# An attention and expert-routing kernel: the first expert's weights asked for ahead of the search's branch, and the logits' update placed behind the row numbers

## The chip, the cores and the metric

The kernel runs on one core of one Trainium2 chip. The metric is the time of one execution in microseconds (us) on the device, as the median of several runs. A profile is one execution more, recorded by the hardware profiler; its times count from the start of the span, the stretch from its first instruction to its last.

## The reference

Two stages follow each other. The first is block-causal attention over 8 batches and 8 heads with 576 positions of 64 numbers; its result is laid out as `x`, 4608 tokens of 512 numbers. The second is a mixture of 8 experts. Each pair (token, expert) has a logit, and the pairs are taken greedily by descending logit: a token goes to one expert, an expert takes at most `cap` = 576 tokens.

```python
logits = x @ w_gate                      # [4608, 8]
order = np.argsort(-logits.flatten())
for idx in order:
    tok, e = (int(idx) // E, int(idx) % E)
    if assigned[tok] >= 0 or counts[e] >= cap:
        continue
    assigned[tok] = e
    counts[e] += 1
for e in range(E):
    h = np.maximum(x[assigned == e] @ w1[e], 0.0)   # w1: 512 x 1024
    out[assigned == e] = h @ w2[e]                  # w2: 1024 x 512
```

## The kernel before

**Order of the work.** Both stages are written as Python generators, which a planner (`Sched`) interleaves when the program is built. Each `yield` names an engine (D VectorE, A ScalarE, T TensorE, G GpSimd, S SyncE's DMA queue), an estimated cost in ns and the events to wait for; the planner keeps a clock of each engine and picks the piece that can start first, by priority where pieces compete. So the costs and events only set the order in which instructions stand on each engine; on the chip each engine runs its own list in order and waits on semaphores.

**The experts one by one.** `Moe` does not sort. For k = 0 to 7 it finds the expert whose cap-th largest remaining logit is highest, hands that expert its tokens and takes them out. Expert k stands for the k-th one in that order, and its number is known only at run time. The steps for one expert:

- `route(k)` searches, for all experts at once, the threshold at which 576 tokens lie above it, in rounds t = 0, 1, 2, …: counting on VectorE (`jk`, L809/L810) and ScalarE (`ja`, L752), a TensorE product that sums over partitions (`tot`, L824), and VectorE again (`sg`, L827). For k = 0 alone, ahead of round 4, a test is put in (L776 to L796). It asks whether the expert with the highest lower bound already has exactly 576 tokens above it. If so, a branch (`tc.If(rv==0)`, closed at L845) skips rounds 4 to 13. With these inputs it is skipped. ScalarE, TensorE and VectorE take part in the branch; SyncE does not.
- Behind the branch VectorE marks the expert's tokens (`sm`, `d2`, `ds`, `MM`, `ge`, L849 to L863), and writes the expert's number to `eidx` (L860). `MM` has two halves: tokens above the threshold, and tokens equal to it, of which only the first are taken.
- Scans (L867) and TensorE products (`po`, L879 to L886) turn the marks into positions; `invert` turns positions into row numbers: `OH`, `OL`, `RH` (L920 to L926), products `pe` (L935), a copy `ixt` (L938), products `ps` (L942) and the copy `ix` (L945), 576 row numbers in five columns.
- `gather` lets GpSimd write five indirect DMAs that fetch the rows of `x` (`xg`, L1007), `flip` turns them with TensorE (`xt`, L1017) and copies them to `X` (L1021 ScalarE, L1022 VectorE), and `ffn` multiplies: `h` (L1057), `HH`/`HL` (L1043/L1045), `y` (L1082/L1086).
- `weights(k)` reads `eidx` on SyncE (`value_load`, L957) and queues eight DMAs of 512 KB there (L993): four pieces of w1, four of w2, called n = 0 to 7. Each piece is split into two 16-bit parts: the high part on ScalarE (L965, or L972 and L976), the low part as the difference of the raw piece and the high part, on VectorE for n < 4 of the first two experts (L967, two inputs in SBUF), else on GpSimd (L978). For k = 0 the fifth piece has an order of its own: GpSimd clears one column (L989) behind the last gather, and the fifth DMA waits for that; the other three queue behind it on SyncE.
- The `late` step (`out` with `full`; L869 to L871, L905 to L907) takes the chosen tokens and the chosen expert out of the logits `Lm` and starts `route(k+1)`. For k < 2 it is put on the planner's list when `RH` has been written (L928).

While the first expert is searched nothing else is left to do: attention is over, and no expert has rows yet. From the second expert on, search and gathers run beside the products of the expert before.

Of the kernel before, what the change touches and what calls it, by code (L numbers as in the profile page):

```python
# [8 lines left out]
F32 = mybir.dt.float32  # L9
# [3 lines left out]
OP = mybir.AluOpType  # L13
# [601 lines left out]
class Moe:  # L615
    def __init__(s,tc,nc,ctx,sc,L,xd,w1,w2,out):
        s.tc,s.nc,s.sc,s.L,s.xd,s.w1,s.w2,s.out=tc,nc,sc,L,xd,w1,w2,out
        s.NT=xd.shape[0]; s.D=w1.shape[1]; s.E=w1.shape[0]; s.F=w1.shape[2]; s.CAP=s.NT//s.E; s.C=s.NT//P
        s.NS=14; s.NSC=6; s.NX=4
        s.IFE=(mybir.EngineType.Activation,mybir.EngineType.PE,mybir.EngineType.DVE)  # L620
        s.cp=ctx.enter_context(tc.tile_pool(name="mcp",bufs=1))
        s.ident=s.cp.tile([P,P],F32,name="mident"); make_identity(nc,s.ident)
        s.am=s.cp.tile([P,8],F32,name="m_am"); s.nam=0; nc.gpsimd.memset(s.am,2.0**-50)
        s.ab=s.cp.tile([P,1],F32,name="m_ab")
        s.vm=s.cp.tile([P,s.C],F32,name="m_vm"); s.nP=s.cp.tile([P,s.C,s.E],F32,name="m_nP"); s.Lr=s.cp.tile([P,s.C,s.E],F32,name="m_Lr")
        s.W={}; s.X={}; s.ix={}; s.half={}; s.ny=0
    def consts(s):
        nc,cp=s.nc,s.cp
        yield G,700
# [82 lines left out]
    def route(s,k):  # L712
# [19 lines left out]
        else:  # L732
# [26 lines left out]


            lo=CB[:,0:1]; nw=s.zero; PBx=PB; more=None
            BC=s.BC[k%2]; f=rp.tile([P,2,8],F32,tag="f",name=f"f{k}"); m1=rp.tile([P,6],F32,tag="m1",name=f"m1{k}"); oh=f[:,1]
            def thresholds():
                ps=s.ps.tile([P,512],F32,tag="rt",name=f"bc{k}")
                th=s.ps.tile([P,512],F32,tag="tot",name=f"th{k}")
# [6 lines left out]
            for t in range(s.NS):  # L772
                w=4.0**-t
                cnt=rp.tile([P,3],F16,tag="cnt",name=f"cn{k}_{t}")
                cand=base
                if t==s.NX and k==0:  # L776
                    yield D,70
                    V.tensor_tensor(CB[:,2:3],lo,nw,op=OP.add)
                    yield T,60
                    th=s.ps.tile([P,512],F32,tag="tot",name=f"tx{k}")  # L780
                    nc.tensor.transpose(th[:,:32],CB[:32,2:3].to_broadcast([32,P]),s.ident[:32,:32]); th=th[:,0:8]
                    yield D,429
                    jk=rp.tile([P,N],F16,tag="jk",name=f"jx{k}")
                    V.tensor_scalar(jk,PB[:,:N],CB[:,2:3],0.0,op0=OP.is_lt,op1=OP.add,accum_out=cnt[:,0:1])
                    yield T,60
                    wn=s.ps.tile([P,512],F32,tag="g",name=f"wn{k}",bufs=4)[:,0:8]
                    nc.tensor.matmul(wn,lhsT=cnt[:,0:1].to_broadcast([P,P]),rhs=s.bo[:,0:8],start=True,stop=True)
                    yield D,600
                    V.tensor_reduce(m1[:,0:1],th,axis=AX.X,op=OP.max)
                    V.tensor_scalar(oh,th,m1[:,0:1],0.0,op0=OP.is_equal,op1=OP.add,accum_out=m1[:,1:2])  # L790
                    V.tensor_scalar(f[:,0],oh,m1[:,1:2],1.0,op0=OP.mult,op1=OP.is_equal)
                    V.scalar_tensor_tensor(f[:,0],wn,float(s.NT-s.CAP),f[:,0],op0=OP.is_equal,op1=OP.mult,accum_out=m1[:,1:2])
                    V.tensor_copy(BC[:,0],th)
                    rv=nc.values_load(m1[0:1,1:2].bitcast(I32),engines=s.IFE,skip_runtime_bounds_check_because="0 or the bits of 1.0")
                    more=s.tc.If(rv==0,preferred_fallthrough_block=False); more.__enter__()
                    sc.lag(1000)  # L796
                if t:
                    cand=rp.tile([P,3],F32,tag="cand",name=f"cd{k}_{t}")
                    yield D,70 if k==0 else 210,('P2',k) if PBx is not PB else None
                    if k==0: V.tensor_tensor(cand[:,2:3],base[:,2:3],nw,op=OP.add)  # L800
                    else:
                        for i in (2,0,1): V.tensor_scalar(cand[:,i:i+1],lo,nw,(i+1)*w,op0=OP.add,op1=OP.add)
                P2=s.P2 if t==s.NSC else None
                sc.add(signs(PBx,cand[:,2:3],cnt,t,P2),0,sc.now+200)
                sc.nolat()
                for i in range(2):
                    yield D,429
                    jk=rp.tile([P,N],F16,tag="jk",name=f"jk{k}_{t}_{i}")
                    if t and k==0: V.scalar_tensor_tensor(jk,base[:,i:i+1].to_broadcast([P,N]),nw,PBx[:,:N],op0=OP.add,op1=OP.is_gt,accum_out=cnt[:,i:i+1])  # L809
                    else: V.tensor_scalar(jk,PBx[:,:N],cand[:,i:i+1],0.0,op0=OP.is_lt,op1=OP.add,accum_out=cnt[:,i:i+1])  # L810
                    if i==0: sc.nolat()
                add=lambda o,a,b: V.tensor_tensor(o,a,b,op=OP.add) if k==0 else V.tensor_scalar(o,a,b,None,op0=OP.add)
                if t: add(lo,lo,nw)
                if P2 is not None:
                    V.tensor_scalar(CB[:,2:3],lo,-1.0,None,op0=OP.mult); sc.set(('nlo',k))
                    lo=CB[:,1:2]; PBx=P2
                if t==s.NS-1: add(CB[:,2:3],CB[:,0:1],lo)
                elif k==0:
                    base=rp.tile([P,3],F32,tag="base",name=f"bs{k}_{t}")
                    V.tensor_scalar(base,s.io3,w/4,lo,op0=OP.mult,op1=OP.add)  # L820
                sc.busy(D,330 if k==0 else 150)
                yield T,30,('sg',k,t)
                tot=s.ps.tile([P,512],F32,tag="tot",name=f"tot{k}_{t}")
                nc.tensor.matmul(tot[:,0:3],lhsT=s.bo,rhs=cnt,start=True,stop=True)  # L824
                yield D,72
                sg=rp.tile([P,4],F32,tag="sg",name=f"sg{k}_{t}")
                V.scalar_tensor_tensor(sg[:,0:3],tot[:,:3],s.NT-s.CAP+0.5,s.wk[:,t:t+1].to_broadcast([P,3]),op0=OP.is_le,op1=OP.mult,accum_out=sg[:,3:4])  # L827
                nw=sg[:,3:4]
                sc.lag(93)
# [15 lines left out]
            if more: more.__exit__(None,None,None)  # L845
# [3 lines left out]
            V.tensor_tensor(sm,BC,oh[:,None,:].to_broadcast([P,4,8]),op=OP.mult)  # L849
            V.tensor_tensor(d2,PV,be(oh),op=OP.mult)  # L850
            yield D,670
            V.tensor_reduce(m1[:,2:6],sm,axis=AX.X,op=OP.add)
            los,lo2s,hi2s,ei=[m1[:,i:i+1] for i in range(2,6)]
            V.tensor_reduce(ds_,d2,axis=AX.X,op=OP.add)
            u=rp.tile([P,8],F32,tag="u8",name=f"u8{k}")
            yield D,420
# [1 line left out]
            ge=rp.tile([P,C],F16,tag="ge",name=f"ge{k}")  # L858
            V.tensor_scalar(ge,ds_,los,lo2s,op0=OP.subtract,op1=OP.is_ge)
            V.tensor_copy(eidx,ei)  # L860
            sc.add(s.weights(k,eidx),1,sc.now)
            yield D,106
            V.tensor_tensor(MM[:,1],ge,MM[:,0],op=OP.subtract)  # L863
        nm=1 if last else 2
        yield D,106*nm
        for i in range(nm):
# [49 lines left out]
    def invert(s,k,L16,h2):  # L916
# [8 lines left out]
        yield D,440 if k<2 else 800  # L925
        V.tensor_tensor(RH[:,0],OH,s.tok,op=OP.mult)  # L926
        if k>1: V.tensor_scalar(RH[:,1],OH,s.pc,None,op0=OP.mult)
        else: sc.add(s.late(),0,sc.now)  # L928
        s.hold(k)
        yield T,350,'rt',('hold',k)  # L930
        tk=sc.take(); ps=s.ps.tile([P,512],F32,tag="rt",name=f"pe{k}")
# [13 lines left out]
        V.tensor_copy(ix,ps[:,:5])  # L945
        sc.set(tk)
        sc.add(s.gather(k,ix),1,sc.now); sc.set(('ix',k))
        if k==0:

            s.wu=s.ps.tile([P,512],F32,tag="g",name="warm",bufs=4)  # L950
            for n in range(s.NWU): nc.tensor.matmul(s.wu,lhsT=s.ones,rhs=OL.rearrange("p a b -> p (a b)")[:,:512],start=True,stop=True)
            sc.free[T]=max(sc.free[T],sc.now)+213*s.NWU+1500
        s.ix[k]=ix
    def weights(s,k,eidx):

        nc=s.nc; wp=s.wp; sc=s.sc
# [23 lines left out]
        for dst,src,nd,wd in ((W,s.w1,4,1024),(Y,s.w2,8,512)):  # L980
            g=1024//wd
            for d in range(0,nd,g):
                if n>=6: yield S,25,'hw',('wc',k,n-6)
                elif k>0: yield S,25,'hw',('wc',k-1,n+2),('fl',1) if k==1 and n>=4 else None
                elif n==4:

                    yield G,60,('gi',0)
                    raw=wp.tile([P,1024],F32,tag="raw",name=f"raw{k}_{wd}_{d}",bufs=6)
                    nc.gpsimd.memset(raw[:,0:1],0.0)  # L989
                    yield S,25,'hw'  # L990
                else: yield S,25,'hw'
                if k or n!=4: raw=wp.tile([P,1024],F32,tag="raw",name=f"raw{k}_{wd}_{d}",bufs=6)
                nc.sync.dma_start(out=raw.rearrange("p (g f) -> p g f",g=g),in_=src[bass.ds(e,1),d*P:(d+g)*P,:].rearrange("o (g p) f -> p (o g) f",p=P))  # L993
                hi=dst[:,0,d:d+g].rearrange("p g f -> p (g f)"); lw=dst[:,1,d:d+g].rearrange("p g f -> p (g f)")
                sc.dma(1456,('wl',k,n))
                sc.add(conv(n,raw,hi,lw,('wc',k,n)),2,sc.now)
                n+=1
    WS=32.0; XS=64.0; NWU=8; NWM=0; GW=1; GS=2; XC=()
# [151 lines left out]
```

## Time and profile before

| what | before |
|---|---|
| median of 3 runs | 793.67 us (792.71 to 794.05) |
| the profiled execution's own time | 791.57 us |
| its span | 789.8 us |
| mean granted TensorE clock in it | 0.975 |
| TensorE matmuls busy in the span | 715.5 us (91%) |
| VectorE, ScalarE, GpSimd busy | 570.4, 539.2, 466.5 us |

The profiled execution is 2.10 us below the median, and 1.77 us of it lie outside its span. Attention's last output DMA is issued at 344.23 us; the first expert's first product stands at 369.24 us. Between the two lies the stretch in which TensorE has almost nothing to do, and in it all of the changed code runs for k = 0.

### The profile page before, as it was taken

The page shows a single profiled execution, that of the slowest core. Times are in us where ns is not written, and L with a number is a line of the kernel's source. Part 1 is how long each engine was busy: PE and PEld are TensorE (multiplying, and loading weights), DVE is VectorE, ACT ScalarE, POOL GpSimd, SP SyncE. Part 2 cuts the span into 40 slices and gives each one's busy share as a digit, 9 for nine tenths or more (in the row PEclk, how much of TensorE's full clock was granted, in tenths as well). Part 3 has the DMA queues.
Part 4 walks back from the last instruction along what each step waited for, and adds up shares of the span by engine and source line. Part 5 has one row for each costly group of instructions (what it writes and reads, how often), then busy time and mean ns, then how long its engine had stood idle before and what let it go on. Part 6 is the DMA issues. An engine that isn't in the chain of part 4 may idle for free.

```text
span 789.8 us, 19021 instructions
## 1 busy us (share of the span) xinstructions
PE 715.5 (91%) x6528; PEld 476.6 (60%) x6528; DVE 570.4 (72%) x2310; ACT 539.2 (68%) x1455; POOL 466.5 (59%) x509
## 2 busy tenths in 40 slices
PE   5779998899989999936998999999999999999995
PEld 3556776667767777724545747647466475574752
DVE  6899798998899889577988978769686793620210
ACT  5788888888988898715836868594975848283210
POOL 5788888898889876413413447373763907764001
PEclk9899999999999999966999999999999999999998
DMA  9879999999998993347026076481926639851001
GB/s 202 160 150 174 214 189 224 172 151 229 205 192 178 216 181 77 91 106 252 23 98 230 8 245 150 176 199 67 279 71 220 145 103 259 260 136 41 21 20 40
DMA packets 244305, 121.51 MB, mean 154 GB/s; under 512 B 200816, under 2 KB 227312, under 8 KB 244208
## 3 DMA queue, kind: packets, MB, share of 16 engines
q1 hardware_dynamic: 238320, 101.42, 56.7%
q0 software_dynamic: 5888, 18.88, 7.6%
q8 instruction: 51, 0.84, 0.4%
q14 instruction: 46, 0.38, 0.2%
HBM read 71.32 MB, written 18.87 MB: 114 GB/s over the span
## 4 chain that ended last, share of the span: by engine, by line
PE 42%; ACT 3%; DMA 3%; DVE 3%; issue 3%; POOL 1%; SPq 0%; POOLq 0%; another core or an unknown queue 0%; ACTq 0%; DVEq 0%
PE h L1057 23%; PE y L1082 15%; PE y L1086 2%; DMA raw<-in_moe_w_dram 1%; DMA out_dram<-yo,ix 1%; DMA xg<-x,ix 1%; POOL xg L1007 1%; ACT W L976 1%; ACT ja L752 1%; ACT raw L972 1%; DVE OL L924 1%; DVE h L897 1%; PE pe L935 1%; PE tot L824 1%; DVE jk L810 0%
## 5 line engine op out<-in xcount | busy, mean ns | idle before, releaser
L438 POOL TENSOR_TENSOR P<-P,m 128x320 f32<-128x320 f32 (+8 forms) x285 | 209.5, 770 | 49.6 <-DVE m L430 32.5
L1057 PE MATMUL h<-X,W 128*128 128x320 f16 (+3 forms) x1536 | 195.7, 286 | 0.6 <-issue 0.4
L1057 PEld LDWEIGHTS <-W 128*128 128x128 f16 x1536 | 142.0, 98 | 44.3 <-issue 4.7
L416 ACT ACTIVATE P<-psb,m 128x576 f32<-128x576 f32 (+8 forms) x288 | 149.5, 543 | 27.5 <-DVE m L409 18.7
L1082 PE MATMUL y<-W,HH 128*128 128x512 f16 x512 | 152.7, 380 | 0.0
L978 POOL TENSOR_TENSOR W<-raw,W 128x1024 f16<-128x1024 f32 x56 | 118.4, 2135 | 41.6 <-ACT W L976 36.0
L405 DVE TENSOR_REDUCE m<-psb 128x1 f32<-128x576 f32 (+8 forms) x288 | 124.8, 480 | 12.3 <-PE psb L380 11.8
L463 PE MATMUL psb<-mident,P 128*128 128x128 f32 x800 | 106.3, 281 | 13.2 <-POOL P L438 5.9
L1073 POOL DMA_INDIRECT out_dram<-yo,ix x40 | 39.3, 982 | 113.7 <-ACT yo L1065 77.5
L380 PEld LDWEIGHTS <-qT 128*64 128x64 f16 x1408 | 76.6, 111 | 43.6 <-issue 28.9
L463 PEld LDWEIGHTS psb<-mident,P 128*128 128x128 f32 x800 | 87.7, 142 | 24.5 <-POOL P L438 8.5
L380 PE MATMUL psb<-kT,qT 128*64 128x288 f16 (+8 forms) x704 | 89.6, 281 | 11.7 <-ACT P L416 10.9
L498 PE MATMUL psb<-PT,V 128*64 128x448 f32 (+5 forms) x776 | 97.2, 388 | 2.3 <-DVE PT L446 1.8
L1043 ACT ACTIVATE HH<-h 128x320 f16<-128x320 f32 (+3 forms) x128 | 52.3, 411 | 67.7 <-PE h L1057 63.3
L1082 PE MATMUL y<-W,HL 128*128 128x512 f16 x256 | 97.2, 380 | 0.0
L1007 POOL DMA_INDIRECT xg<-x,ix x40 | 40.9, 1023 | 83.0 <-DVE ix L945 38.9
L1045 DVE SCALAR_TENSOR_TENSOR HL<-h,HH 128x320 f16<-128x320 f32 (+3 forms) x128 | 56.9, 452 | 42.5 <-ACT HH L1043 39.4
L444 ACT ACTIVATE PT<-psb 128x512 f32<-128x512 f32 (+1 forms) x165 | 82.6, 593 | 4.5 <-PE psb L463 4.4
L380 PE MATMUL psb<-kS,qT 128*64 128x288 f16 (+8 forms) x704 | 82.0, 278 | 1.6 <-DVE kS L350 1.4
L1082 PEld LDWEIGHTS <-HH 128*128 128x128 f16 x512 | 47.0, 98 | 51.9 <-issue 1.3
L972 ACT ACTIVATE raw<-raw 128x512 f32<-128x512 f32 x112 | 67.7, 627 | 4.5 <-DMA raw<-in_moe_w_dram 4.5
L498 PEld LDWEIGHTS psb<-PT,V 128*64 128x64 f32 x776 | 49.5, 137 | 33.4 <-issue 24.4
(216 smaller groups left out, 1044.1 us busy)
## 6 DMA issues: line engine op xcount, KB each, us to landing
raw<-in_moe_w_dram SPq DMA_DIRECT2D x64, 512.0 KB
x<-XR SPq DMA_DIRECT2D x8, 1152.0 KB
kn<-in_k_dram SPq DMA_DIRECT2D x15, 576.0 KB
qn<-in_q_dram SPq DMA_DIRECT2D x15, 576.0 KB
V<-in_v_dram SPq DMA_DIRECT2D x64, 128.0 KB
V<-in_v_dram SPq DMA_DIRECT2D x16, 64.0 KB
xg<-x,ix POOLq DMA_INDIRECT x40
out_dram<-yo,ix POOLq DMA_INDIRECT x40
```

The costliest lines, as they stand in the source:

```text
L380: nc.tensor.matmul(out if len(K1.shape) == 2 else out.rearrange("p (r j) -> p r j", r=2), lhsT=A[:, h, 64 * i:64 * i + 64], rhs=K1, start= ...
L405: nc.vector.tensor_reduce(m[:, 0, c:c + 1], ps[:, o:o + 64 * (i + 1)] if g else s.part(ps, g, i, o), axis=AX.X if g else AX.XY, op=OP.max)
L416: nc.scalar.activation(out, in_, AF.Exp, bias=m[:, 1, c:c + 1], scale=s.ESC, accum_out=m[:, 2, c:c + 1])
L438: nc.gpsimd.tensor_tensor(sl, sl, m[:, 3, c:c + 1].to_broadcast([P, w]), op=OP.mult)
L444: s.nc.scalar.activation(out, in_, AF.Copy)
L463: nc.tensor.transpose(ps[:, a], s.Pb[n % s.NP][:, s.OFF[i] + 128 * j:s.OFF[i] + 128 * j + P], s.ident)
L498: nc.tensor.matmul(ps[64 * h:64 * h + 64, 64 * (i0 - b0):64 * (b1 - b0)], lhsT=vn[:, j, 2 * (n % 2) + h, :], rhs=pt[:, s.PTI[(j, i0)]:s.PT ...
L972: nc.scalar.activation(raw[:,x],raw[:,x],AF.Copy,scale=s.WS)
L978: nc.gpsimd.tensor_tensor(lw,raw,hi,op=OP.subtract)
L1045: nc.vector.scalar_tensor_tensor(HL[:,f,ts],ps,0.0,HH[:,f,ts],op0=OP.max,op1=OP.subtract)
L1057: nc.tensor.matmul(ps,lhsT=W[:,a,d,f*P:f*P+P],rhs=X[:,4*(d//2)+d%2+l,ts],start=(d==0 and n==0),stop=(d==3 and n==2))
L1082: if m<4: nc.tensor.matmul(ps,lhsT=Z[:,f,m*P:m*P+P],rhs=Y[:,a,f],start=(f==n==0),stop=(f==7 and n==2))
```

## The change

It has two parts, and both act on the first expert (the second part on the second one too).

**Early request and early marks.** Ahead of the branch, VectorE now also works out `eidx` and the first half of `MM` as they are if the branch will be skipped, and clears the second half. `MM[:,0]` comes straight from a comparison of `PV` with the lower bounds, which are raised by 16 for the experts that are not the top one. SyncE reads `eidx` and queues the four DMAs of w1 ahead of the branch, in which it now takes part. All that stood between the branch's end and the scans (`sm` to `MM`) moves inside the branch, where it runs only if the test fails, and there the expert is read and the four DMAs are asked for once more, into the same four buffers. The planner's cost of the test's block goes from 600 to 1800.

**The late step.** For k < 2 it goes on the planner's list behind `ix` instead of behind `RH`.

```diff
-        s.IFE=(mybir.EngineType.Activation,mybir.EngineType.PE,mybir.EngineType.DVE)
+        s.IFE=(mybir.EngineType.Activation,mybir.EngineType.PE,mybir.EngineType.DVE,mybir.EngineType.SP)
...
-                    yield D,600
+                    yield D,1800
                     V.tensor_reduce(m1[:,0:1],th,axis=AX.X,op=OP.max)
+                    V.scalar_tensor_tensor(f[:,2],th,m1[:,0:1],s.io8,op0=OP.is_equal,op1=OP.mult)
+                    V.tensor_reduce(ei,f[:,2],axis=AX.X,op=OP.max)
+                    V.tensor_copy(eidx,ei)
                     V.tensor_scalar(oh,th,m1[:,0:1],0.0,op0=OP.is_equal,op1=OP.add,accum_out=m1[:,1:2])
-                    V.tensor_scalar(f[:,0],oh,m1[:,1:2],1.0,op0=OP.mult,op1=OP.is_equal)
-                    V.scalar_tensor_tensor(f[:,0],wn,float(s.NT-s.CAP),f[:,0],op0=OP.is_equal,op1=OP.mult,accum_out=m1[:,1:2])
-                    V.tensor_copy(BC[:,0],th)
+                    V.tensor_scalar(f[:,0],th,m1[:,0:1],16.0,op0=OP.is_lt,op1=OP.mult)
+                    V.tensor_scalar(f[:,2],oh,m1[:,1:2],1.0,op0=OP.mult,op1=OP.is_equal)
+                    V.scalar_tensor_tensor(f[:,2],wn,float(s.NT-s.CAP),f[:,2],op0=OP.is_equal,op1=OP.mult,accum_out=m1[:,1:2])
+                    V.tensor_tensor(f[:,0],f[:,0],th,op=OP.add)
+                    V.tensor_tensor(d2,PV,be(f[:,0]),op=OP.is_ge)
+                    V.tensor_reduce(MM[:,0],d2,axis=AX.X,op=OP.max)
+                    V.memset(MM[:,1],0.0)
+                    s.ask(eidx)
                     rv=nc.values_load(m1[0:1,1:2].bitcast(I32),engines=s.IFE,skip_runtime_bounds_check_because="0 or the bits of 1.0")
                     more=s.tc.If(rv==0,preferred_fallthrough_block=False); more.__enter__()
...
-            if more: more.__exit__(None,None,None)
...
-            sc.add(s.weights(k,eidx),1,sc.now)
+            if k: sc.add(s.weights(k,eidx),1,sc.now)
             yield D,106
             V.tensor_tensor(MM[:,1],ge,MM[:,0],op=OP.subtract)
+            if more:
+                s.ask(eidx); more.__exit__(None,None,None)
+                for n in range(4): sc.ev['wl',0,n]=sc.now+3500+1500*n
+                sc.add(s.weights(0,eidx),1,sc.now)
...
-        else: sc.add(s.late(),0,sc.now)
...
         sc.add(s.gather(k,ix),1,sc.now); sc.set(('ix',k))
+        if k<2: sc.add(s.late(),0,sc.now)
...
+    def piece(s,raw,src,e,d,g):
+        s.nc.sync.dma_start(out=raw.rearrange("p (g f) -> p g f",g=g),in_=src[bass.ds(e,1),d*P:(d+g)*P,:].rearrange("o (g p) f -> p (o g) f",p=P))
+    def ask(s,eidx):
+        e=s.nc.sync.value_load(eidx[0:1,0:1],min_val=0,max_val=s.E-1)
+        if not s.early: s.early=[s.wp.tile([P,1024],F32,tag="raw",name=f"raw0_{n}",bufs=6) for n in range(4)]
+        for n,t in enumerate(s.early): s.piece(t,s.w1,e,n,1)
```

**SyncE's list, from attention's last write to the first w2 piece.** Before, the expert's number is read once, and the eight pieces follow it:

```order
L540 DMA x<-XR_5097 128x9x512
L845 UNCONDITIONAL_BRANCH
L957 TENSOR_LOAD eidx_5267
L957 ISA x2
L993 ISA
L993 DMA raw_1024_0_5558<-in_moe_w_dram 128x1024
```

In the changed kernel the first four pieces stand ahead of the branch (`m_5270` holds the test's result), and the same request stands again inside the skipped block:

```order
L969 TENSOR_LOAD eidx_5267
L969 ISA x2
L966 ISA
L966 DMA raw_0_5362<-in_moe_w_dram 128x1024
L966 ISA
L966 DMA raw_1_5363<-in_moe_w_dram 128x1024
L966 ISA
L966 DMA raw_2_5364<-in_moe_w_dram 128x1024
L966 ISA
L966 DMA raw_3_5365<-in_moe_w_dram 128x1024
L803 TENSOR_LOAD m_5270
L872 COMPARE_AND_BRANCH
```

The read of `eidx` and the w1 requests moved from behind the marks to ahead of the branch; the w2 requests stay where they were, behind a second read of `eidx`.

**VectorE's list, from the copy `ixt` on.** Before, the six steps of the update (`m_es` to the second `m_Lm`) stand ahead of `ixt0`, and two of the four conversions of w1 behind `ix0`:

```order
L926 TENSOR_TENSOR RH0_5570<-OH0_5569,m_tok_590 128x720
L869 TENSOR_TENSOR m_es_645<-m_es_645,m10_5270 128x1
L870 TENSOR_SCALAR u80_5531<-f0_5269 128x8
L871 TENSOR_TENSOR m_Lm_644<-m_Lm_644,u80_5531 128x288
L905 TENSOR_TENSOR q0_5554<-q0_5554,MM0_5265 128x36
L906 TENSOR_SCALAR q0_5554<-q0_5554 128x36
L907 TENSOR_TENSOR m_Lm_644<-m_Lm_644,q0_5554 128x288
L938 CAST ixt0_5621<-pe0_5584 128x40
L945 CAST ix0_5633<-ps0_5624 128x5
L967 SCALAR_TENSOR_TENSOR W1_0_5545<-raw0_1024_0_5558,W1_0_5545 128x1024
L967 SCALAR_TENSOR_TENSOR W1_0_5545<-raw0_1024_1_5563,W1_0_5545 128x1024
L721 TENSOR_REDUCE m_vm_75<-m_Lm_644 128x36
```

In the changed kernel the same steps read so (L880 to L882 and L916 to L918 are the update):

```order
L948 CAST ixt0_5646<-pe0_5609 128x40
L955 CAST ix0_5657<-ps0_5648 128x5
L880 TENSOR_TENSOR m_es_645<-m_es_645,m10_5270 128x1
L881 TENSOR_SCALAR u80_5556<-f0_5269 128x8
L882 TENSOR_TENSOR m_Lm_644<-m_Lm_644,u80_5556 128x288
L916 TENSOR_TENSOR q0_5592<-q0_5592,MM0_5265 128x36
L917 TENSOR_SCALAR q0_5592<-q0_5592 128x36
L918 TENSOR_TENSOR m_Lm_644<-m_Lm_644,q0_5592 128x288
L985 SCALAR_TENSOR_TENSOR W1_0_5584<-raw0_0_5362,W1_0_5584 128x1024
L985 SCALAR_TENSOR_TENSOR W1_0_5584<-raw0_1_5363,W1_0_5584 128x1024
L985 SCALAR_TENSOR_TENSOR W1_0_5584<-raw0_2_5364,W1_0_5584 128x1024
L721 TENSOR_REDUCE m_vm_75<-m_Lm_644 128x36
```

The update moved behind `ix0`, and three conversions of w1 instead of two stand in one piece behind it.

More of the change, by code (lines that the diff above doesn't have):

```diff
@@ L625, in __init__ @@
         s.vm=s.cp.tile([P,s.C],F32,name="m_vm"); s.nP=s.cp.tile([P,s.C,s.E],F32,name="m_nP"); s.Lr=s.cp.tile([P,s.C,s.E],F32,name="m_Lr")
-        s.W={}; s.X={}; s.ix={}; s.half={}; s.ny=0
+        s.early=[]; s.W={}; s.X={}; s.ix={}; s.half={}; s.ny=0
     def consts(s):
@@ L761, in route @@
             lo=CB[:,0:1]; nw=s.zero; PBx=PB; more=None
-            BC=s.BC[k%2]; f=rp.tile([P,2,8],F32,tag="f",name=f"f{k}"); m1=rp.tile([P,6],F32,tag="m1",name=f"m1{k}"); oh=f[:,1]
+            BC=s.BC[k%2]; f=rp.tile([P,3,8],F32,tag="f",name=f"f{k}"); m1=rp.tile([P,6],F32,tag="m1",name=f"m1{k}"); oh=f[:,1]
+            los,lo2s,hi2s,ei=[m1[:,i:i+1] for i in range(2,6)]; d2=R("d2")
             def thresholds():
@@ L844, in route @@
             V.tensor_scalar(oh,f[:,0],m1[:,1:2],None,op0=OP.is_equal)
-            if more: more.__exit__(None,None,None)
             sm=rp.tile([P,4,8],F32,tag="sm",name=f"sm{k}")
-            d2=R("d2"); ds_=rp.tile([P,C],F32,tag="ds",name=f"ds{k}")
+            ds_=rp.tile([P,C],F32,tag="ds",name=f"ds{k}")
             yield D,463
@@ L852, in route @@
             V.tensor_reduce(m1[:,2:6],sm,axis=AX.X,op=OP.add)
-            los,lo2s,hi2s,ei=[m1[:,i:i+1] for i in range(2,6)]
             V.tensor_reduce(ds_,d2,axis=AX.X,op=OP.add)
@@ L982, in weights @@
             for d in range(0,nd,g):
-                if n>=6: yield S,25,'hw',('wc',k,n-6)
+                if k==0 and n<4: raw=s.early[n]
+                elif n>=6: yield S,25,'hw',('wc',k,n-6)
                 elif k>0: yield S,25,'hw',('wc',k-1,n+2),('fl',1) if k==1 and n>=4 else None
@@ L991, in weights @@
                 else: yield S,25,'hw'
-                if k or n!=4: raw=wp.tile([P,1024],F32,tag="raw",name=f"raw{k}_{wd}_{d}",bufs=6)
-                nc.sync.dma_start(out=raw.rearrange("p (g f) -> p g f",g=g),in_=src[bass.ds(e,1),d*P:(d+g)*P,:].rearrange("o (g p) f -> p (o g) f",p=P))
+                if k or n>4: raw=wp.tile([P,1024],F32,tag="raw",name=f"raw{k}_{wd}_{d}",bufs=6)
+                if k or n>3: s.piece(raw,src,e,d,g)
                 hi=dst[:,0,d:d+g].rearrange("p g f -> p (g f)"); lw=dst[:,1,d:d+g].rearrange("p g f -> p (g f)")
-                sc.dma(1456,('wl',k,n))
+                if k or n>3: sc.dma(1456,('wl',k,n))
                 sc.add(conv(n,raw,hi,lw,('wc',k,n)),2,sc.now)
```

## The prediction, made before the run

> **What bounds the kernel now.** The page comes first: TensorE's busy time in the span.
>
> ```profile
> PE 715.5 (91%) x6528; PEld 476.6 (60%) x6528; DVE 570.4 (72%) x2310; ACT 539.2 (68%) x1455; POOL 466.5 (59%) x509
> ```
>
> TensorE bounds the whole, so the change can only act where it has nothing to do: between attention's end and the first expert's products. There I read the chain that ended last, from 355 to 376 us, then the timelines of the engines, and then what TensorE waits for afterwards. The chain (start, duration, piece):
>
> ```profile
> 355.20 0.48 SPq L957
> ...
> 356.29 3.56 DMA raw<-in_moe_w_dram
> ...
> 360.07 1.07 ACT W L965
> ...
> 369.43 4.83 DMA raw<-in_moe_w_dram
> 374.29 0.63 ACT raw L972
> ...
> 375.08 0.55 ACT ja L752 x2
> ```
>
> It runs through two transfers of weights: the first piece of w1, asked for at 356.29, and later a piece of w2, issued at 369.43. Between them stand GpSimd's five gathers, of which this is the timeline:
>
> ```profile
> 361.20 1.18 POOL L1007 DMA_INDIRECT xg<-x,ix  x1 [15.87 <-ACT W L965]
> 362.69 1.73 POOL L1007 DMA_INDIRECT xg<-x,ix  x1 [0.30 <-issue]
> 364.72 0.95 POOL L1007 DMA_INDIRECT xg<-x,ix  x1 [0.30 <-issue]
> 365.97 1.53 POOL L1007 DMA_INDIRECT xg<-x,ix  x1 [0.30 <-issue]
> 367.81 0.91 POOL L1007 DMA_INDIRECT xg<-x,ix  x1 [0.30 <-issue]
> 368.71 0.12 POOL L989 MEMSET raw<- 128x1 f32 x1
> ```
>
> Read literally, the first gather waits for ScalarE's conversion of w1, so that an earlier w1 would start the gathers 3.7 us earlier. I don't believe that label: a gather needs only the row numbers `ix`. VectorE's timeline and the line's own waits decide:
>
> ```profile
> 350.56 0.16 DVE L789 TENSOR_REDUCE m<-tx 128x1 f32<-128x8 f32 x1
> ...
> 351.46 0.16 DVE L793 COPY m_BC<-tx 128x8 f32<-128x8 f32 x1
> 353.35 0.19 DVE L849 TENSOR_TENSOR sm<-m_BC,f 128x32 f32<-128x32 f32 x1 [1.73 <-DVEq L845]
> ...
> 354.86 0.14 DVE L860 CAST eidx<-m 128x1 int32<-128x1 f32 x1
> ...
> 355.08 0.35 DVE L867 TENSOR_TENSOR_SCAN SC<-m_ones,MM 128x36 f16<-128x36 f16 x2
> ...
> 358.15 0.15 DVE L869 TENSOR_TENSOR m_es<-m_es,m 128x1 f32<-128x1 f32 x1
> ...
> 359.24 0.46 DVE L907 TENSOR_TENSOR m_Lm<-m_Lm,q 128x288 f32<-128x288 f32 x1
> 359.62 0.19 DVE L938 CAST ixt<-pe 128x40 f16<-128x40 f32 x1
> 360.15 0.16 DVE L945 CAST ix<-ps 128x5 int32<-128x5 f32 x1 [0.35 <-PE ps L942]
> 361.16 2.42 DVE L967 SCALAR_TENSOR_TENSOR W<-raw,W 128x1024 f16<-128x1024 f32 x2 [0.84 <-ACT W L965]
> ...
> 365.45 1.23 DVE L967 SCALAR_TENSOR_TENSOR W<-raw,W 128x1024 f16<-128x1024 f32 x1 [1.01 <-ACT W L965]
> ```
>
> ```profile
> L1007 POOL DMA_INDIRECT xg<-x,ix x40: 907/963/1942, 361.2 to 690.9; - x40
> L1007 POOLq EVENT_SEMAPHORE  x31: 17/17/10703, 342.9 to 686.7; - x31
> ```
>
> GpSimd's queue held one wait of 10.70 us. GpSimd had been idle for 15.87, since 345.3, and `ix` ends at 360.31. A wait for `ix` fits, and 0.89 behind it the first gather starts. So the stretch is set by the chain VectorE to `ix`, then by five gathers one after the other (361.20 to 368.72, 7.52 us), then by w2 behind the last gather. TensorE shows what follows:
>
> ```profile
> 358.29 0.92 PE L935 MATMUL pe<-RH,OL 128*32 128x40 f16 x36 [2.56 <-DVE RH L926]
> ...
> 366.30 1.42 PE L1017 MATMUL xt<-m_idh,xg 128*128 128x128 f16 x16 [2.67 <-DMA xg<-x,ix]
> 368.41 1.03 PE L1017 MATMUL xt<-m_idh,xg 128*128 128x128 f16 x8 [0.69 <-DMA xg<-x,ix]
> ...
> 375.68 0.16 PE L824 MATMUL tot<-cn,m_bo 128*128 128x3 f16 x1 [1.42 <-DVE HL L1045]
> ```
>
> ```profile
> PE xt L1017 <- DMA xg<-x,ix: 2.0, 2, 1.8
> PE tot L824 <- DVE jk L810: 1.6, 2, 1.1
> PE pe L935 <- DVE RH L927: 1.4, 1, 1.4
> ```
>
> The second fence holds TensorE's largest waits from 376 to 790 us (total, times, longest). They are small, so behind the product `tot` at 375.68, the second round of the second expert's search, TensorE works nearly without a gap, and whatever moves that `tot` moves the end. It waits there for `ja` (375.08 + 0.55 = 375.63), which on ScalarE stands behind the conversion at 374.29, that is behind w2.
>
> **The change part by part.** The sum is made against the profiled execution, 791.57 us, and carried over to the median, 793.67.
>
> *The request.* `eidx` now needs three small steps behind the reduction at 350.56. At the pitch of such steps (353.35 to 355.08 holds eight steps, two of them on 288 columns) they take about 0.6, so it stands at about 351.4 instead of 355.00. From there to the first request went 1.29 (355.00 to 356.29); kept, this gives 352.7, 3.6 earlier, and the first piece lands near 356.2 instead of 359.85. This alone buys little: its readers are the conversions, and they are not what the gathers waited for. W1's own queue stays the same; w2 still stands behind the last gather, and the second read of `eidx` ahead of it finds SyncE idle.
>
> *The marks.* Behind the branch eight steps go: 353.35 to 355.08, 1.73. Ahead of it come two steps on 288 columns, like two of the eight, and five small ones net of the copy that goes, about 1.6. VectorE sat idle 1.73 between the copy and `sm`, waiting for the branch's value; part of the new steps stands behind the value, so up to 0.4 can lie beside that wait. Net −0.1 to −0.5; I take −0.15. SyncE's part in the branch costs nothing while it waits for no one but the same value: behind it lies only w2, 15 us later.
>
> *The late step.* `pe` ends at 359.21, but `ixt` starts at 359.62, since VectorE is in the update from 358.15 to 359.70 (the records overlap by a pipeline). With `ixt` free to go it starts near 359.25: −0.35. Together `ix` is 0.5 earlier (0.35 to 0.85), ending near 359.8, and the first gather starts near 360.7 by the same 0.89.
>
> *What the update and the conversions now collide with.* The median of the forty gathers is 0.963, but two of the first five took 1.73 and 1.53. Both started inside a conversion on VectorE: at 362.69 in the pair 361.16 to 363.58, and at 365.97 in the one 365.45 to 366.68. They ended 0.84 and 0.82 after that conversion's end. So such a gather waits until the conversion is over. The two that began with no conversion under way took 0.95 and 0.91. The first, recorded 0.04 behind a conversion's start, took 1.18: the edge isn't sharp. The Trainium skill, page "SBUF — State Buffer", section "Who interferes with whom", says that a VectorE operation with two SBUF inputs and a GpSimd operation that reads SBUF exclude each other for a whole instruction, and that issue order decides who waits; both rows agree, and the rule too gives one waiting gather per conversion that is under way when it is issued.
>
> In the changed kernel the update starts behind `ix`, 1.55 long (358.15 to 359.70 before), to about 361.35. The three conversions follow in one piece, 3 × 1.21 (half of 2.42) to 365.0, since w1 has landed and ScalarE has converted ahead. The gathers start at 360.7. The first (0.96) ends at 361.65; the second starts at 361.95 inside the first conversion, waits to 362.55 and ends 0.83 later, 363.4; three more at 0.30 + 0.963 each end at 367.2. Before it was 368.72: −1.5. The last conversion stands behind `X` and out of the gathers' way. W2 is issued 1.5 earlier, and the search's own branch (`PV`, `rt` behind the fourth `xt`) moves by the fourth gather's end, also about 1.5 earlier. So `tot` moves from 375.68 to about 374.2.
>
> Sum: −0.5 from `ix`, −1.0 from one stretched gather instead of two. The profiled execution would be 790.07, and the median 792.17. Its bounds: `ix` by −0.35 or −0.85 and the waiting gather by ±0.4 give −0.9 to −2.3.
>
> **The rivals.** About 0.2% of this kernel, 1.59 us, is what a measurement can tell from no change.
>
> *A, the conversions do not let GpSimd in (18%).* Three stand back to back. That a loser waits through several is seen with the engines exchanged:
>
> ```profile
> L897 DVE TENSOR_SCALAR h<-q x8: 174/182/5274, 356.3 to 669.2; 128x36 f16<-128x36 f32 x8
> ```
>
> ```profile
> 668.11 6.30 POOL L978 TENSOR_TENSOR W<-raw,W 128x1024 f16<-128x1024 f32 x3
> ```
>
> A step of VectorE whose median is 0.18 took 5.27 from 669.2 on, to the end of three operations of GpSimd (674.4). If so here, the second gather waits to 365.0, ends at 365.8, and three more end at 369.6: +0.9, 794.6. Against it: no row shows GpSimd locked out over a boundary between two VectorE operations.
>
> *B, the first gather is caught too (12%).* This is the other side. The last update step has two inputs in SBUF as well and starts at about 361.35 − 0.46 = 360.9. If the first gather, due at 360.7, comes 0.2 later relative to it, and boundaries are closed as in A, it waits to 365.0, ends at 365.8, and four more (4 × 1.263) end at 370.9: +2.2, 795.9. The point that decides is whether the gather reads ahead of 360.9.
>
> *F, the branch's instructions come late (8%).* Ahead of `sm` the chain has a piece in which VectorE waits for nothing that is shown:
>
> ```profile
> 352.84 0.52 issue
> ```
>
> No weight moves there now; w1 will. What a busy machine adds is seen in a gather's way to TensorE: the first took 361.20 to 366.30, 5.10, under w1; the third 364.72 to 368.41, 3.69; the second expert's first took even more:
>
> ```profile
> 414.36 1.00 POOL L1007 DMA_INDIRECT xg<-x,ix  x1 [4.42 <-DVE ix L945]
> ```
>
> ```profile
> 421.12 0.62 PE L1017 MATMUL xt<-m_idh,xg 128*128 128x128 f16 x8 [1.78 <-DMA xg<-x,ix]
> ```
>
> That is 6.76. Added to the chain, 1.4 to 3.1 would leave −0.1 to +1.6, say 794.4. Against it: w1's data starts about when the branch is taken. The Trainium skill, page "Runtime: NRT & Kernel Launch", section "Instruction fetch mechanics", says that a taken branch to a page not held must fetch it by DMA first; the 0.52 may be such a fetch, which no run here shows.
>
> *G, more than forecast (12%).* If no gather is caught (the first two get between the update and the conversions), five take 5 × 0.963 + 1.2 = 6.0, which is −2.0 with `ix`; and the second expert's wait of 1.78 at 421.12 may shrink by some 0.4 with its update moved: −2.4, 791.3.
>
> That the test fails is no case: the same inputs skip the block now, in the 1.73 ahead of `sm`.
>
> **How the numbers follow.** The forecast has 50%. Its own range, −0.9 to −2.3, straddles the limit of 1.59, so 24 of its 50 count as faster, 26 as the same. G adds 12 to faster; A gives 13 same and 5 slower; B 12 slower; F 4 and 4. That makes 0.36 faster, 0.43 same, 0.21 slower. The time is the forecast's, 792.2. The range goes down to 790.8, which holds most of G, and up to 795.3, which holds A and F and leaves out most of B.
>
> **What would show it.** Right: the first w1 request near 352.7; `ixt` straight behind `pe`; `ix` near 359.8; the gathers' end near 367.2 with only the second stretched, to about 1.45; `tot` near 374.2; and from there the same distance to the end as before. A shows as a second gather of about 3.8, B as a first one of about 5, F as a piece of "issue" behind the branch of over 1 us. It is wrong if the first gather starts 3 us earlier (then the label at 361.20 was right), or if `tot` moves and the end does not.

## The result: slower, and not where the change was made

| | before | after |
|---|---|---|
| median | 794.43 us (10 runs, 792.71 to 798.34) | 800.85 us (10 runs, 798.9 to 802.21) |
| ratio | | 1.0071, 95% interval 1.0049 to 1.0092 |
| profiled execution, span | 791.57, 789.8 us | 800.26, 798.2 us |

The change costs about 0.7%. The forecast was a small gain, and the range ended at 795.3; it was wrong. To find the place I set both traces against marks that lie in both. The first is the product `tx`, attention's work being over and the test just beginning; it stands 0.60 later in the profile after, a difference that arose in attention, which the change does not touch. The last mark is the product `tot` on which the prediction rested. Before and after:

```profile
350.06 0.31 PE L781 MATMUL tx<-mident,CB 32*128 32x32 f32 x1 [0.46 <-DVE CB L778]
```

```profile
350.66 0.31 PE L782 MATMUL tx<-mident,CB 32*128 32x32 f32 x1 [0.46 <-DVE CB L779]
...
375.93 0.16 PE L833 MATMUL tot<-cn,m_bo 128*128 128x3 f16 x1 [1.51 <-ACT ja L752]
```

From `tx` to `tot` it was 25.62 (350.06 to 375.68) and is 25.27: the stretch that the change edits became 0.35 shorter. From `tot` to the end of the span it was 414.1 and is 422.3. All the loss, some 8 us in this pair of executions (the medians are 6.4 apart), lies behind the edited code. TensorE's waits there show it. These are the groups in the profile after, from 376 us to the end (total, times, longest); the first holds the 1.51 at 375.93 too:

```profile
PE tot L833 <- ACT ja L752: 7.8, 6, 2.3
PE tot L833 <- DVE jk L819: 2.9, 2, 2.1
PE pe L945 <- DVE RH L938: 2.7, 1, 2.7
PE xt L1036 <- DMA xg<-x,ix: 2.3, 3, 1.7
PE h L1076 <- DMA X<-xg: 1.0, 1, 1.0
```

With 0.3 of small ones that is 17.0, or 15.5 without 375.93; before it was 6.9. The difference, 8.6, is about the loss of this pair. It is one execution of each kernel, and not every wait in it belongs to the order of the lists, as will be seen. The worst place is the turn from the second expert's last products `y` to the third one's first `h`. In the timeline of the profile after, TensorE stands in front of four things in a row:

```profile
475.90 0.38 PE L1101 MATMUL y<-W,HL 128*128 128x512 f16 x1
478.39 0.18 PE L833 MATMUL tot<-cn,m_bo 128*128 128x3 f16 x1 [2.11 <-DVE jk L819]
...
482.73 0.16 PE L833 MATMUL tot<-cn,m_bo 128*128 128x3 f16 x1 [1.18 <-ACT ja L752]
483.87 0.50 PE L1076 MATMUL h<-X,W 128*128 128x256 f16 x3 [0.98 <-DMA X<-xg]
484.94 0.16 PE L833 MATMUL tot<-cn,m_bo 128*128 128x3 f16 x1 [0.56 <-ACT ja L752]
```

Before, the same turn has no wait at all:

```profile
478.41 0.18 PE L824 MATMUL tot<-cn,m_bo 128*128 128x3 f16 x1
...
479.62 0.38 PE L1086 MATMUL y<-W,HL 128*64 128x512 f16 x2
479.94 0.83 PE L1057 MATMUL h<-X,W 128*128 128x256 f16 x6
480.60 0.17 PE L824 MATMUL tot<-cn,m_bo 128*128 128x3 f16 x1
```

Behind these waits the clock is halved. In the windows of the profile after, the first number is the length, then comes the busy time of TensorE; the granted clock stands ahead of the DMA share. In the same three windows of the profile before it was 1.00:

```profile
480.00:484.50 4.50, 2.21 (x17) 0.77 (x13) 3.42 (x23) 4.48 (x12) 4.50 (x3) 1.00 1.05 324
484.50:488.00 3.50, 3.06 (x16) 2.29 (x17) 2.56 (x15) 3.48 (x10) 3.30 (x3) 0.51 1.31 205
488.00:492.00 4.00, 4.00 (x40) 3.58 (x39) 2.69 (x16) 3.13 (x9) 4.00 (x3) 1.00 0.16 56
```

Twenty-four `h` took 4.25 there (484.96) instead of 2.78 (482.96 before), 1.5 more. In the balance of this pair that does not show, since the kernel before has such a stretch near 422 to 425 us (0.74 from 420 to 424, 0.84 from 424 to 428), where the changed one has 1.00.

**What stands there.** The lists of the engines show what the waits mean. Between `rt`, the start of the fourth expert's search, and the first `h` of the third expert, TensorE's list holds these pieces (`y*3` is three pieces of the second expert's products, 0.65 us each; `T` a search product `tot`):

```
before  rt  y*3 T  y*3 T  y*4 T  y*3 T  y*4 T  y*3 T  y*2 h h T  h*7 T
after   rt  y*4 T  y*3 T  y*3 T  y*4 T  y*3 T  y T  h T  h*8 T
```

Before, 22 pieces of `y` were left behind `rt`; now 18 are, since the search of the third expert and all that follows on it stands later on the list. The fifth and sixth round had 7 pieces together to hide behind and now have 4, and the seventh, which had 4 (two `y`, two `h`), has one `h`. A round needs VectorE's and ScalarE's turn of about 2 us (from the `tot` at 480.62 to the next at 482.73, 2.11). With one piece between two `T`, TensorE stands in front of the second.

The first wait of the four, 2.11 at 478.39, is another matter: four pieces stand ahead of that `tot`, enough for a round. VectorE's step `sg`, which reads the `tot` of 473.50, starts only at 476.73, while in the next three rounds it starts 0.2 behind the start of its `tot`:

```profile
476.73 0.16 DVE L836 SCALAR_TENSOR_TENSOR sg<-tot,m_wk 128x3 f32<-128x3 f32 x1 [3.22 <-PE y L1101]
```

Another such late start (524.92, for the `tot` of 522.19) stands ahead of the longest wait behind, 2.27 at 526.60. The kernel before has one too (519.87, for the `tot` of 518.26), so have e5 to e8 below, and e1 to e4 and e9 to e12 have none. What held `sg` is open.

### The profile page after: what moved, and what is told of

It is laid out like the page before. It is cut to its first block, busy times and chain, and to the rows that moved or that the text cites. A ratio compares the mean times of both kernels' runs of the same rounds, so it can differ in the third digit from the quotient of the medians.

```text
span 798.2 us, 19036 instructions
## 1 busy us (share of the span) xinstructions
PE 719.1 (90%) x6528; PEld 479.6 (60%) x6528; DVE 571.5 (72%) x2309; ACT 540.4 (68%) x1455; POOL 465.4 (58%) x509
## 4 chain that ended last, share of the span: by engine, by line
PE 59%; DVE 17%; ACT 8%; DMA 7%; POOL 4%; issue 4%; SPq 0%; POOLq 0%; DVEq 0%; ACTq 0%
PE h L1076 23%; PE y L1101 17%; PE psb L463 6%; DVE m L405 5%; PE psb L498 5%; PE psb L380 4%; ACT P L416 4%; DMA kT<-k 3%; DMA raw<-in_moe_w_dram 2%; DVE kS L350 2%; PE y L1105 2%; POOL P L438 2%; ACT PT L444 1%; DVE PT L446 1%; POOL xg L1026 1%
## 5 line engine op out<-in xcount | busy, mean ns | idle before, releaser
L438 POOL TENSOR_TENSOR P<-P,m 128x320 f32<-128x320 f32 (+8 forms) x285 | 209.5, 770 | 49.9 <-DVE m L430 32.8
L380 PE MATMUL psb<-kT,qT 128*64 128x288 f16 (+8 forms) x704 | 91.7, 286 | 10.4 <-ACT P L416 9.8
L380 PE MATMUL psb<-kS,qT 128*64 128x288 f16 (+8 forms) x704 | 83.8, 283 | 1.4 <-DVE kS L350 1.2
L498 PEld LDWEIGHTS psb<-PT,V 128*64 128x64 f32 x776 | 49.7, 138 | 33.1 <-issue 24.3
```

Of the source, the lines that this page charges most:

```text
L380: nc.tensor.matmul(out if len(K1.shape) == 2 else out.rearrange("p (r j) -> p r j", r=2), lhsT=A[:, h, 64 * i:64 * i + 64], rhs=K1, start= ...
L438: nc.gpsimd.tensor_tensor(sl, sl, m[:, 3, c:c + 1].to_broadcast([P, w]), op=OP.mult)
L498: nc.tensor.matmul(ps[64 * h:64 * h + 64, 64 * (i0 - b0):64 * (b1 - b0)], lhsT=vn[:, j, 2 * (n % 2) + h, :], rhs=pt[:, s.PTI[(j, i0)]:s.PT ...
```

## The experiments

All ratios are against the kernel before, run in the same set on the same chip; its median was 788.94, 796.49 and 789.52 us in the three sets (e1 to e4, e5 to e8, e9 to e12), so times of different sets are not compared. A profile is one execution each time, and the kernel before was not profiled again in these sets. There were two groups of theories: the loss is in the order of the lists behind the seam (O), or the seam itself leaves something slow behind (S).

### e1 and e2: the order moved from one kernel to the other

The planner was made to follow a list of pieces written down from the other kernel, from the product at 375.93 on; the second expert's late step stands where that list needs it.

```diff
+            if s.replay and not s.replay_off:
+                x = min(c, key=lambda y: s.rank.get(s.label(y[3]), -1))
             k, e, cost = x[3], x[5], x[6]
+            l = s.label(k)
...
+            if l == s.SWITCH:
+                s.replay = True
```

e1, the change with the order of before. 

> The changed kernel up to the second expert's second search product (tot of round 1), from there on the order of the kernel before on all engines; the second expert's late step is back behind RH, since that order asks for it. Theory O (the 8 us are lost to the order in which the planner places all that follows): TensorE's waits from 376 us on fall from about 15 us to the 7 of before, and the time is that of before less the 0.3 gained at the seam, ratio 0.997 to 1.002. Theory S (the seam does it: the early w1 transfers, the request or the clock leave something slow behind): the time stays at that of the changed kernel, ratio 1.007.

e2, the kernel before with the order of the change. 

> The mirror image: the kernel before, with its own request and marks, but from the second expert's second search product on in the order of the changed kernel; the second expert's late step therefore stands behind ix. Theory O: as slow as the changed kernel, ratio 1.006 to 1.011, with the same waits of TensorE near 478 to 485, 526, 620, 627 and 690 us. Theory S: ratio 1.000.

Measured: e1 1.0003 (0.9984 to 1.0022), e2 1.0088 (1.0059 to 1.0116). The loss goes with the order and not with the seam. e2 shows the same place, here with a longer wait for `X`, and again half clock behind it:

```profile
484.00 0.18 PE L848 MATMUL tot<-cn,m_bo 128*128 128x3 f16 x1 [0.93 <-DVE jk L834]
487.00 0.82 PE L1082 MATMUL h<-X,W 128*128 128x256 f16 x3 [2.83 <-DMA X<-xg]
```

```profile
480.00:486.00 6.00, 3.25 (x28) 1.38 (x26) 4.89 (x31) 5.69 (x14) 5.80 (x4) 1.00 0.84 220
486.00:493.00 7.00, 6.00 (x30) 4.26 (x31) 2.47 (x12) 4.63 (x12) 6.80 (x5) 0.51 1.01 220
```

The turn's two waits (0.93 and 2.83) and the 3.4 us that 7.00 us at 0.51 lose make 7.2, an estimate from these rows; the loss is 0.88% of 788.94, 6.9. So here the turn is about the whole loss. Of the other waits expected, one came (1.31 at 627.74); there is none at 526 or 620, and the one near 690 is 1.27, as in the kernel before (1.37). So the wait at 526 and what the one at 690 grew by in the profile after (2.27, and 2.67 instead of 1.37) do not follow from the order alone: e2 has the same lists there.

e1 has no wait between 430 and 567 us. Its waits came down to 9.8 and not to 7, as expected, because of one of 3.83 at 617.35, in a part whose lists are those of before:

```profile
617.35 0.16 PE L857 MATMUL tot<-cn,m_bo 128*128 128x3 f16 x1 [3.83 <-ACT ja L776]
```

The kernel before waited 0.77 at the like place. ScalarE's row says what this `ja` stands behind on its list, a conversion whose weights had not landed:

```profile
616.12 0.63 ACT L1015 ACTIVATE raw<-raw 128x512 f32<-128x512 f32 x1 [4.15 <-DMA raw<-in_moe_w_dram]
```

So a wait of that kind varies between executions of one order.

### e3 and e4: the two parts of the change alone

e3 is the kernel before with the late step behind `ix` for both experts:

```diff
-        else: sc.add(s.late(),0,sc.now)
...
+        if k<2: sc.add(s.late(),0,sc.now)
```

> The kernel before with the second part of the change alone: the late step behind ix for the first two experts, request and marks as before. Theory O: this is the part that upsets the order (the third expert's search is started later), so ratio 1.006 to 1.011. Theory S: ratio 0.999 to 1.001.

e4 is the changed kernel with that edit undone. 

> The changed kernel with the late step back behind RH for both experts: early request, early marks and the new cost alone. Theory O: the order of GpSimd's list is that of before, so ratio 0.998 to 1.003. Theory S: ratio 1.007.

Measured: e3 1.0083 (1.0055 to 1.0111), all of the loss. e4 1.0044 (1.0015 to 1.0073): a miss, neither the one nor the other. GpSimd's list is that of before, but TensorE's differs up to the fourth expert's tenth round. From 401 us on all four engines' lists are those of e6 and e10 below, which do not lose, so the order behind that is not what costs here. Its profile has a wait like that of e1, 2.77 at 620.76, behind weights that landed late, but e1 had it too and lost nothing. What e4's 0.4% is stays open.

### e5 and e6: which of the two late steps

e5 is the kernel before with the second expert's late step alone moved (`if k==1` behind `ix`), e6 the changed kernel with that step alone put back:

```diff
+        elif k==1: sc.add(s.late(),0,sc.now)
...
-        if k<2: sc.add(s.late(),0,sc.now)
+        if k<1: sc.add(s.late(),0,sc.now)
```

> The kernel before with one edit: the second expert's late step stands behind its row numbers instead of behind RH; the first expert's stretch is untouched. The third expert's search then starts about 3 us later, and GpSimd again has a scatter of the second expert ahead of the third one's gathers. Theory O1 (this step alone upsets the order behind it): ratio 1.005 to 1.010, with waits of TensorE between 478 and 490 us and a stretch of half clock behind them. Theory O2 (the planner's clock, set off by any edit at the seam, is what reshuffles the order): 0.999 to 1.002.

> The changed kernel with the second expert's late step back behind RH, the planner left to itself. Theory O1: the loss goes, ratio 0.997 to 1.004 (the request alone gave 1.004). Theory O2: ratio 1.006 to 1.009.

Measured: e5 1.0066 (1.0035 to 1.0097), e6 0.9980 (0.9958 to 1.0002). So the trigger is the second expert's late step, an edit that does not touch the first expert's stretch. In e5 that stretch is as before, and the waits between 478 and 490 us are there: 0.68, 0.93 and, for `X`, 0.97. The half clock that was expected behind them did not come: it was 1.00 from 480 to 492 us.

```profile
480.00:486.00 6.00, 4.10 (x36) 2.06 (x36) 4.96 (x31) 5.69 (x14) 5.98 (x4) 1.00 0.99 269
```

### e7 and e8: is it GpSimd's list?

In the profile after, GpSimd's gathers for the third expert start at 469.33, though the row numbers are there at 466.41: a scatter stands ahead of them.

```profile
468.06 0.96 POOL L1092 DMA_INDIRECT out_dram<-yo,ix  x1 [7.06 <-ACT m_PB L747]
469.33 0.98 POOL L1026 DMA_INDIRECT xg<-x,ix  x1 [0.30 <-issue]
```

This looked like the cause. e7 moves that one scatter behind the gathers in the changed kernel, e8 moves the gathers behind it in the kernel before; both by an edit of the list of pieces. For e7, of GpSimd's pieces:

```diff
-yev.1.1.128#2 gather.2#1 gather.2#2 gather.2#3 gather.2#4 gather.2#5
+gather.2#1 gather.2#2 gather.2#3 gather.2#4 gather.2#5 yev.1.1.128#2
```

> The changed kernel with one instruction moved on GpSimd's list: the scatter of the second expert's second output tile stands behind the third expert's five gathers instead of ahead of them; all other lists are the same. The gathers then start near 466.6 instead of 469.3. Theory G (this scatter is where the time goes: gathers late, X late, waits near 484): the wait for X near 484 goes and the time falls by 2 to 5 us against the changed kernel, ratio to before 1.001 to 1.005. Theory P (it is TensorE's list: search products that stand too late among the expert products): within 1 us of the changed kernel, ratio 1.006 to 1.009.

> The kernel before with the five gathers of the third expert moved on GpSimd's list behind the second expert's second scatter (and one conversion), nothing else moved: they start near 473 instead of 464.7. Theory G: X comes 8 us later than before, TensorE waits for it several us near 480 to 486 and loses half clock behind that: ratio 1.006 to 1.015. Theory P: there is slack of that size, ratio below 1.003.

Measured: e7 1.0062 (1.0039 to 1.0086), e8 1.0038 (1.0011 to 1.0065). e7 did what it was to do on GpSimd and bought nothing that can be measured; its ratio is in the range of theory P. Its gathers start early, the wait for `X` is gone, and TensorE waits in front of `tot` instead:

```profile
465.42 0.98 POOL L1050 DMA_INDIRECT xg<-x,ix  x1 [5.66 <-DVE bs L715]
```

```profile
474.32 0.18 PE L857 MATMUL tot<-cn,m_bo 128*128 128x3 f16 x1 [1.91 <-DVE jk L843]
...
480.99 0.18 PE L857 MATMUL tot<-cn,m_bo 128*128 128x3 f16 x1 [0.93 <-DVE jk L843]
...
483.17 0.16 PE L857 MATMUL tot<-cn,m_bo 128*128 128x3 f16 x1 [1.66 <-DVE CB L848]
```

So my first explanation (late gathers) fell for the changed kernel: without the late gathers the loss stays. What is left is TensorE's own list, where the rounds stand with too few products to hide them. That is argued from the waits and the count of pieces; no run moved the rounds alone, and the 1.91 follows a late start of `sg` (472.64, for the `tot` of 470.28), which the list does not explain. e8 lies between its two ranges, a miss for both: gathers that come 8 us late cost 0.4%, less than expected, but not nothing.

### e9 to e12: where in the order, and can it be better?

e9 follows the changed kernel's order up to the fourth expert's first `tot` and the order of before from there. 

> The changed kernel in its own order, the late third expert's search included, up to the first search product of the fourth expert (about 469 us); from there on the order of the kernel before. Theory P1 (the late search itself costs: row numbers, gathers and X of the third expert come too late for TensorE): the loss stays, ratio 1.005 to 1.010. Theory P2 (only the arrangement behind it is bad): ratio 0.998 to 1.002.

e10 repeats e6. 

> The kernel of the request and the first late step once more, since its gain stood at the edge of the interval. If the seam's gain carries to the end: ratio 0.996 to 0.999. If not: 0.999 to 1.002.

e11 puts the second expert's late step further ahead still:

```diff
-            if k>1: sc.add(out(),0,sc.now)
+            if k>0: sc.add(out(),0,sc.now)
...
-        if k<2: sc.add(s.late(),0,sc.now)
+        if k<1: sc.add(s.late(),0,sc.now)
```

> As the run before, but the second expert's late step goes still further ahead, to where the third and later experts have it (before OH). Theory P1 (the search is a chain to be started as early as possible): a little faster than the run before, ratio 0.995 to 0.999. If TensorE has slack for it already: the same as the run before; if VectorE's step in front delays the second expert's own row numbers by its 1.5 us: 1.000 to 1.003.

e12 moves the first expert's late step alone. 

> The kernel before with only the first expert's late step behind its row numbers. It frees ixt by 0.35 us and moves the update in front of the conversions. Expected from the seam alone: ratio 0.999 to 1.001, and no new wait of TensorE behind 430 us.

Measured: e9 1.0040 (1.0011 to 1.0069), e10 1.0008 (0.9982 to 1.0034), e11 1.0184 (1.0146 to 1.0221), e12 0.9998 (0.9973 to 1.0023).

e9 lies between its two theories, and its interval reaches into both, so the time alone decides nothing; its profile is read below. e10 takes back e6's hint of a gain, and e12 came out as expected. e11 is the largest miss of all: earlier is not better. There one wait of 8 us holds TensorE in the third expert's first products, for a conversion of w1 on GpSimd:

```profile
480.57 1.36 PE L1076 MATMUL h<-X,W 128*128 128x256 f16 x11
489.96 1.04 PE L1076 MATMUL h<-X,W 128*128 128x256 f16 x4 [8.04 <-POOL W L996]
```

GpSimd's timeline there shows why: the conversion stands behind a scatter that waits 7 us itself:

```profile
478.76 1.01 POOL L1092 DMA_INDIRECT out_dram<-yo,ix  x1 [0.17 <-issue]
486.80 0.96 POOL L1092 DMA_INDIRECT out_dram<-yo,ix  x1 [7.03 <-DMA X<-xg]
487.78 6.28 POOL L996 TENSOR_TENSOR W<-raw,W 128x1024 f16<-128x1024 f32 x3
```

It is the same kind of cause in another list: the planner placed pieces in an order in which one that is not ready holds up one that is needed. What that scatter itself waited for I did not test; the label is the trace's. Nor did the chain come earlier on the chip: the update ends 1.3 us earlier than in e10 (410.16 instead of 411.45), but the search's first product `rt` stands later (415.21 instead of 414.29), and so do the second expert's row numbers (414.69 instead of 413.17). No version here beats the kernel before by what a measurement can tell.

**All traces together.** The profiles show where the time goes. I take the time from the second expert's first `h` to the fourth's, which spans the turn and the stretch behind it. First the kernel before, then the changed one:

```profile
430.11 1.81 PE L1057 MATMUL h<-X,W 128*128 128x256 f16 x15
...
531.32 1.16 PE L1057 MATMUL h<-X,W 128*128 128x256 f16 x9
```

```profile
429.48 0.50 PE L1076 MATMUL h<-X,W 128*128 128x256 f16 x3
...
538.28 0.50 PE L1076 MATMUL h<-X,W 128*128 128x256 f16 x3
```

That makes 101.2 and 108.8 us. The same distance in the other profiles, set by set:

| set | with the second late step behind `RH` | behind `ix`, or in its order | otherwise moved |
|---|---|---|---|
| e1 to e4 | e1 99.7, e4 99.6 | e2 106.7, e3 105.9 | |
| e5 to e8 | e6 101.9 | e5 104.5, e7 107.1 | e8 109.2 |
| e9 to e12 | e10 99.6, e12 99.8 | e9 103.6 | e11 113.9 |

So 7.6 of the 8.2 us of before and after lie in these 100 us, and each kernel that loses by this step is 2.6 to 7 us longer there than the unharmed ones of its set. In e9 it is the turn alone: from the second to the third expert's first `h` 53.8, where e10 has 49.7, and from there to the fourth's 49.8 and 49.9. Behind `rt` the lists that do not lose have 22 pieces of `y` left (e1) or 24 (e6, e10, e12), and those of e2, e3, e5, e7 and e9 18 or 19.

A single profile's waits are no measure of a loss. e6 and e10 are the same program, and neither is slower than the kernel before of its set; TensorE's waits behind 377 us are 13.0 us in the one and 7.2 in the other.

## Why the prediction was wrong, step by step

Times are counted from `tx`, since that stands 0.60 later in the profile after. The rows of that profile that answer to the prediction's:

```profile
361.04 1.18 POOL L1026 DMA_INDIRECT xg<-x,ix  x1 [15.10 <-DMA raw<-in_moe_w_dram]
362.52 1.09 POOL L1026 DMA_INDIRECT xg<-x,ix  x1 [0.30 <-issue]
363.92 1.96 POOL L1026 DMA_INDIRECT xg<-x,ix  x1 [0.30 <-issue]
...
367.44 0.91 POOL L1026 DMA_INDIRECT xg<-x,ix  x1 [0.30 <-issue]
```

```profile
355.24 0.36 DVE L878 TENSOR_TENSOR_SCAN SC<-m_ones,MM 128x36 f16<-128x36 f16 x2 [1.42 <-DVEq L872]
...
359.99 0.17 DVE L955 CAST ix<-ps 128x5 int32<-128x5 f32 x1 [0.35 <-PE ps L952]
...
361.56 3.50 DVE L985 SCALAR_TENSOR_TENSOR W<-raw,W 128x1024 f16<-128x1024 f32 x3
```

```profile
353.26 0.38 SPq L966
...
369.11 5.57 DMA raw<-in_moe_w_dram
374.70 0.63 ACT raw L990
375.33 0.55 ACT ja L752 x2
```

- **The request: right.** First w1 request forecast 2.64 behind `tx` (352.7), measured 2.60. And it moved no gather, as forecast: the label at the first one changed from ScalarE to the w1 transfer, and the gather still starts 0.88 behind `ix`.
- **The marks and `ixt`: right, the first a little undersized.** From `tx` to the scans 4.58 instead of 5.02, −0.44 where −0.15 was taken and −0.5 was the bound. From the scans to the end of `ix` 4.92 instead of 5.23, −0.31 where −0.35 was forecast. Together −0.75, inside the −0.35 to −0.85.
- **The gathers: mechanism right, sum wrong.** The second was caught and ended at 363.61, 0.83 behind the first conversion's end (362.78), as forecast, while the conversions ran on: rival A, the closed boundary, is refuted, and so is B. But the third started at 363.92, 0.08 behind the third conversion's start (363.84), and was caught whole: 1.96, to 0.82 behind that conversion's end at 365.06. Again two stretched gathers instead of one. By the prediction's own numbers the third was due at 363.7 and the third conversion at 361.35 + 2 × 1.21 = 363.8; the sum took the free side of this close call and put no price on the other. The first gather was mis-sized as well: it took 1.18 again, now with no conversion under way, where 0.96 was taken. It takes 1.18 in thirteen of the fourteen traces, so the prediction was wrong to read that length as a blurred edge. The five took 7.31 (361.04 to 368.35) against 7.52: −0.2 where −1.0 was forecast.
- **W2: not forecast.** It was issued 0.92 earlier counted from `tx`, but its landing took 5.57 instead of 4.83. That leaves −0.18 for the conversion behind it. The other 0.17 has nothing to do with w2: a piece `HH` of that length stood between the conversion and `ja` before, and now stands behind `ja`. So of the forecast −1.5 at `tot`, −0.35 was left, half of it by luck.
- **"Whatever moves that `tot` moves the end": this step failed.** It took for granted that behind `tot` the same lists run as before. They do not: in the changed kernel the planner rearranges them up to the fifth expert's first products, and in e4 and e12 up to the third's. The prediction gave what lies behind `tot` no term but a gain of 0.4 in G. It was some 8 us the other way in the profiles (0.7% over all runs), where the whole seam was worth 1.5 by the forecast; e1, e2, e3 and e5 show that the second expert's late step and the order that follows from it cost this. None of the rivals had it either: A and B lie at the seam and did not come, and F shows no sign, since VectorE's wait for the branch is 1.42, where it was 1.73.

The prediction did name the sign of its own failure: `tot` moves and the end does not follow.

What stays open: what holds `sg` up in some executions, what of the turn's cost is TensorE's list and what the late `X`, and what costs e4 its 0.4%.

## What to carry to other kernels

Where a planner sets the lists, an edit's largest effect may lie far behind it: compare the lists to their end, and count at each turn how many pieces of the bound engine's work hide each step of a latency chain (here 22 pieces left before, 18 after). A local gain can be separated from such a rearrangement by making the planner follow a written list; the transplant both ways (e1 and e2) settled in one set what no reading of the seam could. And putting a chain's start earlier on a list is no remedy by itself: e11 did, and lost more than twice as much.

## What the runs showed of the hardware

- Half clock without a long pause: from 475.9 to 484.5 us no wait of TensorE exceeded 2.11 us, and it was busy 2.21 of the last 4.50; the granted clock still fell to about half for the next 3.5 us, in which 24 `h` took 1.5 us more than before. In e2 it fell after 3.25 busy of 6.00. It did not fall in e5 (4.10 of 6.00, 480 to 486 us) nor in e7 (3.41 of 6.00, 478 to 484 us), so where the limit lies is open.
- A gather that begins as little as 0.07 us behind the start of a two-input VectorE operation is held for all of it (1.96 instead of 0.95), but one that waits gets in between two such operations that stand back to back (1.09). The first of before, 0.04 behind one, was not held: 1.18 is its length in thirteen of the fourteen traces. In all of them the gathers recorded from 0.07 to 1.0 us behind a conversion's start ended 0.78 to 0.86 behind its end (1.05 in one case, a first gather, which is longer by 0.23), and none recorded 0.04 or less behind its start was held. So the edge is sharp, and it lies between the two.
